# One core, attention then two expert stages: q's tail is loaded a step later and turned into features beside its own attention

## The chip, the cores and the metric

The kernel runs on one core of a Trainium2 chip. The metric is the device time of the whole program in microseconds, the median of three runs. The core has a matrix engine (PE; PEld is its weight load), a vector engine (DVE), an activation engine (ACT), GpSimd (POOL) and a queue engine (SP) that here only issues transfers.

## What is computed

Attention with random features on 2 batches, 8 heads, 576 positions and 64 dimensions (128 features), then a gated layer, then four experts. The attention part, which is the one touched, is:

```python
def phi(x):                       # x is q or k, scaled by D**-0.25
    proj = np.einsum('bhsd,md->bhsm', x, omega)
    h = proj - np.sum(x * x, axis=-1, keepdims=True) / 2.0
    h = h - np.max(h, axis=-1, keepdims=True)
    return np.exp(h) / np.sqrt(m)
kv = np.einsum('bhsm,bhsd->bhmd', k_p, v)
z = np.sum(k_p, axis=2)
num = np.einsum('bhsm,bhmd->bhsd', q_p, kv)
den = np.einsum('bhsm,bhm->bhs', q_p, z)[..., None] + 1e-06
return num / den
# then, on tokens x = attention, heads side by side:
h = (x @ w1) * (x @ w2) @ w3 @ w_out
out = sum over e of p[:, e] * (relu(h @ ew1[e]) @ ew2[e])
```

## The kernel before

Two heads of one batch make a pair; there are eight pairs, numbered 0 to 7, and pairs 0 to 3 are batch 0. Of the 576 positions of a head, 512 are the main part. The 64 that are left, of both batches together, make the tail: 128 rows by 8 heads, one tile for k, one for q, two for v.

The loop from line 514 runs nine steps. In step n the features of pair n are made (`features_k`, `features_q`), pair n-1 is finished (`kv_sums`, `transpose_e`, `attend`, `place`), pair n+1 is transposed (`transpose_kq`) and pair n+2 is loaded. The features of half a pair are one product on PE into a bank `ps_f` (line 279), a maximum on DVE (line 285) and four exponentials on ACT (line 291). Line 316 has the exponentials of pairs 5 to 7, which use `features_halves`. A transposed input goes from the bank `ps_t` to `kT` by DVE or to `qT` by ACT; the features of q (`eq`) are transposed into the one bank `ps_et` and copied to `eT` by ACT.

The tail has its own functions. `tail_k` makes features `ekt` in step 0. `tail_q` (line 489) makes those of q, transposes them and leaves them in `eTt`; it is called in step 1. `attend_tail` (line 458) uses `eTt` after the last pair of each batch, that is in steps 4 and 8. In both raw tiles of the tail, `tail_raw`, the tag is `xs`, which has two buffers and is also the tag of the attention results that `attend` makes.

Beside the attention, under lower priority, each step runs pieces of the table `BESIDE` (line 41): `o` loads one tile of the output weights (`wo`, eight in all, in steps 0 to 2), `f0` to `f7` fold `w3` with `wo` (line 195, from step 2 on; each fold is two transposed halves and twice twelve products), and `w` and `b` are weights and products of the gated layer. Weights lie in memory as 64-bit numbers. `from_f64` loads them into one of three buffers `f64`, and turns them into 32 bits with one ACT instruction (line 93) and two DVE instructions (lines 94 and 95); `split` makes two parts, by ACT (line 80) and by POOL or DVE (line 81).

A scheduler that runs when the program is built sets the order on each engine from the priorities and its own idea of durations. Each engine then runs its list in that order and waits at the head of it.

Of the kernel before, what the change touches and what calls it, by code (L numbers as in the profile page):

```python
# [8 lines left out]
F32 = mybir.dt.float32  # L9
# [36 lines left out]
def attention_moe_kernel(ctx: ExitStack, tc: tile.TileContext, q, k, v, omega, mw1, mw2, mw3, mwo, probs, ew1, ew2, out):  # L46
    nc = tc.nc
    B, H, S, D = q.shape
# [3 lines left out]
    NE, _, EFF = ew1.shape  # L52
    P = 128
    NPAIR = H // 2
    R = 4
# [19 lines left out]
    def bank(tag):  # L75
        return ps_p.tile([P, 512], F32, tag=tag, name="ps_" + tag, bufs=BANKS[tag])
# [31 lines left out]
    def transpose(out, in_, rows=slice(0, P)):  # L108
        return nc.tensor.transpose(out, in_, ident[rows, rows])
# [27 lines left out]
    def load_w12(g):  # L137

        for w, src in enumerate((mw1, mw2)):
            src = src[:, g * P:(g + 1) * P].rearrange("(k p) c -> p k c", p=P)  # L140
            t = load_w64(w1_p, src, "w12", nc.gpsimd)
            w12[w, g] = t.rearrange("p a (k c) -> p a k c", k=KD)

    def load_wo():
        f = len(wo)
        wo.append(load_w64(w1_p, mwo[f * P:(f + 1) * P].unsqueeze(1), "wo", nc.gpsimd))
# [38 lines left out]
    def fold(m):  # L185

        po = bank("po")
        n = 0
        for hf in range(KF // 4):
            u = m * (KF // 4) + hf  # L190
            while len(w3T) < min(u + 2, KF * (KF // 4)):
                fold_transposed(len(w3T))
            for g in range(4):
                for a, c in PASSES:
                    nc.tensor.matmul(  # L195
                        out=po, lhsT=w3T[u][:, a, g * P:(g + 1) * P], rhs=wo[hf * 4 + g][:, c],
                        start=(n == 0), stop=(n == 3 * KF - 1),
                    )
                    n += 1
        t = w3_p.tile([P, 2, 512], F32R, tag="w3o", name="w3o", bufs=KF)  # L200
        split(t[:, HI], t[:, LO], po)
        w3o.append(t)
# [51 lines left out]
    with ExitStack() as actx:  # L254
        at = actx.enter_context(tc.tile_pool(name="at", bufs=2))
# [3 lines left out]
        def transposed(r, name, tag="t"):  # L259

            ps = bank(tag)
            for g in range(4):
                transpose(ps[:, g * P:(g + 1) * P], r[:, 2 * g:2 * g + 2].rearrange("p r d -> p (r d)"))
            t = at.tile([P, 512], F32, tag=name, name=name)
            if name == "kT":
                nc.vector.tensor_scalar(out=t, in0=ps, scalar1=SCALE, scalar2=None, op0=ALU.mult)
            else:
                nc.scalar.activation(out=t, in_=ps, func=ACTF.Copy, scale=SCALE)
            return t
# [3 lines left out]
        def features(t, half, e, tag="f", wide=False):  # L273


            ps = bank(tag)
            for g in range(2):
                c = (half * 2 + g) * P
                nc.tensor.matmul(
                    out=ps[:, g * 256:(g + 1) * 256], lhsT=t[:, c:c + P], rhs=om.rearrange("p j m -> p (j m)"),  # L280
                    start=True, stop=True,
                )
            pv = ps.rearrange("p (g m) -> p g m", m=M)
            mx = at.tile([P, 4], F32, tag="mx", name="mx", bufs=4)
            top = nc.vector.tensor_reduce(out=mx, in_=pv, op=ALU.max, axis=AX.X, negate=True)
            if wide:
                nc.vector.tensor_tensor(out=e, in0=pv, in1=mx.unsqueeze(2).to_broadcast([P, 4, M]), op=ALU.add)
                last = nc.scalar.activation(out=e, in_=e, func=ACTF.Exp)
            else:
                for g in range(4):  # L290
                    last = nc.scalar.activation(out=e[:, g], in_=pv[:, g], func=ACTF.Exp, bias=mx[:, g:g + 1])
            ended.append(last.ins)
            return top.ins, last.ins
# [26 lines left out]
        def load_tail(r, src, b, eng=nc.sync):  # L320
            eng.dma_start(out=r, in_=src[b, :, MAIN:, :].rearrange("h s d -> s h d"))
# [12 lines left out]
        rows_of = [slice(b * TAIL, (b + 1) * TAIL) for b in range(B)]  # L334
# [123 lines left out]
        def attend_tail(b, ps_of):  # L458

            rows = rows_of[b]  # L460
            xs = at.tile([P, H, D], F32, tag="xs", name="xs")
            for f in range(2):
                ps = bank(("x", "kv")[f])
                for g in range(4):
                    h = f * 4 + g
                    nc.tensor.matmul(
                        out=ps[:, g * D1:(g + 1) * D1], lhsT=eTt[:, h], rhs=ps_of[h // 2].kva[:, h % 2],
                        start=True, stop=True,
                    )
                normalised(xs[:, f * 4:(f + 1) * 4], ps, slice(0, P), 4)  # L470
            ps = bank("et")
            s = TAIL_COLS
            for i in range(NPAIR):
                transpose(ps[:, i * P:(i + 1) * P], xs[:, 2 * i:2 * i + 2].rearrange("p j d -> p (j d)"))
            for i in range(NPAIR):
                x, c = xt[b][i], i * P + b * TAIL
                split(x[:, HI, s], x[:, LO, s], ps[:, c:c + TAIL])
# [3 lines left out]
        def pair(n):  # L481
            return pairs[n] if 0 <= n < len(pairs) else None

        def tail_k():
            t = transposed(tail_raw[0], "kT")
            for half in range(2):
                features(t, half, ekt[:, half * 4:half * 4 + 4])

        def tail_q():
            t = transposed(tail_raw[1], "qT")  # L490
            for half in range(2):
                e = at.tile([P, R, M], F32, tag="eq", name="eq", bufs=3)
                features(t, half, e)
                ps = bank("et")
                for g in range(4):
                    transpose(ps[:, g * P:(g + 1) * P], e[:, g])
                nc.scalar.activation(
                    out=eTt[:, half * 4:half * 4 + 4], in_=ps.rearrange("p (g t) -> p g t", g=4), func=ACTF.Copy,
                )

        pairs[0].load_kq(nc.scalar)
        with tc.issue_after(om_first):
            pairs[0].transpose_kq()
        tail_raw = [at.tile([P, 2 * R, D], F32, tag="xs", name="tail") for _ in range(2)]
        for b in range(B):
            load_tail(tail_raw[0][rows_of[b]], k, b)
        pairs[0].load_v()
# [6 lines left out]
        for n in range(len(pairs) + 1):  # L514
            u, u1, nx, nx2 = pair(n), pair(n - 1), pair(n + 1), pair(n + 2)
            with tc.high_priority(offset=-100 if n < 6 else 400):
                if u:
                    u.place_v()
                if n == 0:
                    for b in range(B):  # L520
                        load_tail(tail_raw[1][rows_of[b]], q, b)
                if nx2:
                    nx2.load_kq()
                    nx2.load_v()
                    loaded = nx2.loaded
                if u1:
                    u1.kv_sums()
                if u:
                    u.features_k()
                if u1:  # L530
                    u1.transpose_e(0)
                    u1.transpose_e(1)
                if u:
                    u.features_q()
                if n == 0:
                    tail_k()
                if u1:
                    u1.attend()
                if n == 1:
                    tail_q()  # L540
                if nx:
                    nx.transpose_kq()
                if u1:
                    u1.place()
                    if u1.i == NPAIR - 1:
                        attend_tail(u1.b, pairs[u1.n - u1.i:u1.n + 1])
            with ExitStack() as order:

                for ins in (*u.mark, loaded) if u else ():
                    order.enter_context(tc.issue_after(ins))  # L550
                for s in BESIDE.get(n, "").split():
                    if s[0] == "w":
                        load_w12(int(s[1]))
                    elif s[0] == "o":
                        load_wo()
                    elif s[0] == "f":
                        fold(int(s[1]))
                    else:
                        gated(at, 2, int(s[1]), int(s[2]), ("w", "po") * 2)
# [319 lines left out]
```

## Time and profile before

| what | us |
|---|---|
| median of 3 runs | 675.74 (674.23 to 676.59) |
| profiled execution, own time | 675.28 |
| its span, first to last instruction | 673.5 |
| PE busy in the span | 661.3 (98%) |
| ACT busy | 414.1 (61%) |
| DVE busy | 448.9 (67%) |

The span holds four stages: attention with the weights that are prepared beside it, the folds and the first gated products that join it from 59 us on, the rest of the gated layer, and from about 310 us the experts. A busy share is a mean over stages with different limits. So the rows that count are those of the stage that the change touches, and in it the times at which PE has nothing to do. Busy time of PE is drawn a little long, since the ends of products are modelled; the distance from the start of one row to the start of the next is what tells whether PE ran on.

### The profile page before, as it was taken

Reading aid. Unit: us, or ns where it says so; the run is one execution under the profiler, and the core shown is the slowest. Engines: PE = TensorE matmul, PEld = TensorE weight load, DVE = VectorE, ACT = ScalarE, POOL = GpSimd, SP = SyncE. Lnnn points to the kernel's source line nnn. Section 1 sums busy time; section 2 is a strip of 40 time slices with the busy share of each in tenths; the row PEclk is TensorE's granted clock in tenths of the full one; section 3 lists DMA queues with packets and bytes.
Section 4 is the critical chain, followed back from the end, with each engine's and each line's share of the span. In section 5 each row is a group of like instructions: output and inputs, shape, how many; then the busy total and the mean of one; then the engine's idle time right before and its main releaser. Section 6 shows DMA issues by size and latency. Waiting matters only on the chain.

```text
span 673.5 us, 12392 instructions
## 1 busy us (share of the span) xinstructions
PE 661.3 (98%) x4895; PEld 634.7 (94%) x4895; DVE 448.9 (67%) x754; ACT 414.1 (61%) x895; POOL 123.9 (18%) x145
## 2 busy tenths in 40 slices
PE   8999999999999999999999999999999999999997
PEld 6788888889999999999899999999999998999996
DVE  3867755657462225257968867968689588687795
ACT  5897465574352224237868778768587677687740
POOL 2321000042140000000022141321331312304300
PEclk9999999999999999999999999999999999999999
DMA  9865333156120002002255385592872765737715
GB/s 230 289 204 173 109 111 95 63 176 200 32 64 1 1 1 64 1 1 64 77 143 142 46 145 108 98 154 48 156 142 32 147 120 83 142 75 105 135 44 172
DMA packets 51178, 70.58 MB, mean 105 GB/s; under 512 B 8048, under 2 KB 34160, under 8 KB 51120
## 3 DMA queue, kind: packets, MB, share of 16 engines
q1 hardware_dynamic: 37792, 49.05, 24.3%
q0 software_dynamic: 12640, 20.19, 20.1%
q8 instruction: 38, 0.62, 0.4%
q10 hardware_dynamic: 688, 0.56, 0.2%
q14 instruction: 20, 0.16, 0.1%
HBM read 47.24 MB, written 22.54 MB: 104 GB/s over the span
## 4 chain that ended last, share of the span: by engine, by line
PE 83%; DMA 5%; DVE 4%; issue 3%; ACT 3%; SPq 1%; POOL 0%; DVEq 0%; ACTq 0%; POOLq 0%
PE ps_po L195 6%; PE ps_f L709 6%; PE ps_f L791 5%; PE ps_x L709 3%; PE ps_w L709 3%; PE ps_et L709 3%; PE ps_po L158 3%; PE ps_f L158 3%; PE ps_kv L709 3%; PE ps_po L709 3%; PE ps_kv L791 3%; PE ps_x L791 3%; PE ps_w L158 3%; PE ps_et L791 3%; PE ps_t L709 2%
## 5 line engine op out<-in xcount | busy, mean ns | idle before, releaser
L743 POOL DMA_DIRECT2D out_dram<-o x98 | 81.9, 912 | 355.2 <-DVE o L768 173.0
L81 DVE TENSOR_TENSOR hs<-hd,hs 128x1024 fp32r<-128x1024 f32 x48 | 58.3, 1218 | 1.5 <-ACT hs L80 1.5
L80 ACT ACTIVATE hs<-hd 128x1024 fp32r<-128x1024 f32 x48 | 50.6, 1056 | 5.7 <-DVE hd L605 4.6
L195 PE MATMUL ps_po<-wo,w3T 128*128 128x512 f32 x192 | 48.3, 400 | 0.0
L709 PE MATMUL ps_f<-x,w1e 128*128 128x288 f32 x288 | 46.2, 294 | 0.0
L693 ACT ACTIVATE hd<-hd 128x288 f32<-128x288 f32 x96 | 40.7, 438 | 9.0 <-DVE hd L691 8.5
L605 DVE TENSOR_TENSOR hd<-hd 128x512 f32<-128x512 f32 x64 | 43.9, 686 | 0.8
L605 DVE TENSOR_TENSOR raw<-raw 128x512 f32<-128x512 f32 x64 | 43.9, 686 | 0.5
L791 PE MATMUL ps_f<-w2e,hs 128*128 128x256 f32 x288 | 43.2, 282 | 0.0
L81 DVE TENSOR_TENSOR w2e<-raw,w2e 128x1024 fp32r<-128x1024 f32 x32 | 38.8, 1218 | 5.4 <-ACT w2e L80 5.3
L195 PEld LDWEIGHTS ps_po<-wo,w3T 128*128 128x128 f32 x192 | 34.8, 188 | 7.0
L709 PEld LDWEIGHTS ps_f<-x,w1e 128*128 128x128 f32 x288 | 40.9, 188 | 0.1
L791 PEld LDWEIGHTS ps_f<-w2e,hs 128*128 128x128 f32 x288 | 38.5, 191 | 0.1
L80 ACT ACTIVATE w2e<-raw 128x1024 fp32r<-128x1024 f32 x32 | 33.1, 1054 | 6.3 <-DVE raw L605 3.2
L81 POOL TENSOR_TENSOR w<-w12f,w 128x512 fp32r<-128x512 f32 x16 | 23.5, 1478 | 68.0 <-ACT w L80 68.0
L81 DVE TENSOR_TENSOR w1e<-raw,w1e 128x1024 fp32r<-128x1024 f32 x24 | 29.3, 1219 | 5.8 <-ACT w1e L80 5.7
L158 PE MATMUL ps_po<-xt,w 128*128 128x288 f32 x144 | 32.5, 296 | 0.4 <-DVE w3o L81 0.4
L158 PE MATMUL ps_w<-xt,w 128*128 128x288 f32 x144 | 32.8, 297 | 0.0
L80 ACT ACTIVATE hid<-a 128x288 fp32r<-128x288 f32 x32 | 12.8, 439 | 28.8 <-DVE a L169 28.8
L80 ACT ACTIVATE w1e<-raw 128x1024 fp32r<-128x1024 f32 x24 | 25.4, 1058 | 6.2 <-issue 2.6
L94 DVE TENSOR_SCALAR f64e<-f 128x512 uint32<-128x512 uint32 x40 | 20.6, 520 | 8.4 <-DMA f<-in_moe_w_dram 5.5
L158 PE MATMUL ps_x<-xt,w 128*128 128x288 f32 x96 | 25.8, 297 | 0.0
(272 smaller groups left out, 1769.2 us busy)
## 6 DMA issues: line engine op xcount, KB each, us to landing
f<-in_moe_w_dram SPq DMA_DIRECT2D x32, 512.0 KB, 3.8
raw<-in_moe_w_dram SPq DMA_DIRECT2D x32, 512.0 KB, 5.2
out_dram<-o POOLq DMA_DIRECT2D x56, 256.0 KB, 5.3
out_dram<-o POOLq DMA_DIRECT2D x42, 128.0 KB, 4.8
f<-in_moe_w_out_dram SPq DMA_DIRECT2D x8, 512.0 KB, 6.2
kr<-in_k_dram SPq DMA_DIRECT2D x8, 256.0 KB, 5.3
vr<-in_v_dram SPq DMA_DIRECT2D x8, 256.0 KB, 4.9
o<-out_dram SPq DMA_DIRECT2D x8, 256.0 KB, 3.8
```

The lines of the kernel that those rows point to most:

```text
L80: nc.scalar.activation(out=hi, in_=src, func=ACTF.Copy)
L81: (eng or nc.vector).tensor_tensor(out=lo, in0=src, in1=hi.bitcast(F32), op=ALU.subtract)
L94: nc.vector.tensor_scalar(out=e, in0=low, scalar1=29, scalar2=None, op0=ALU.logical_shift_right)
L158: nc.tensor.matmul(out=bs[c][:, :HS], lhsT=w12[w, g][:, x, kk], rhs=xt[b][kk][:, y, c * HS:(c + 1) * HS], start=(kk == 0 and n == 0), stop ...
L195: nc.tensor.matmul(out=po, lhsT=w3T[u][:, a, g * P:(g + 1) * P], rhs=wo[hf * 4 + g][:, c], start=(n == 0), stop=(n == 3 * KF - 1),)
L605: nc.vector.tensor_tensor(out=o, in0=x, in1=y, op=op)
L693: nc.scalar.activation(out=h, in_=src, func=ACTF.Relu)
L709: nc.tensor.matmul(out=ps, lhsT=w1t[a][:, x, kk, g * P:(g + 1) * P], rhs=x2[b, kk][:, y, s], start=(k in "125" and kk == 0 and n == 0), st ...
L743: dma = nc.gpsimd.dma_start(out=out[toks, d], in_=src[rows], **({} if fresh else dict(accum_op=ALU.add))).ins
L791: nc.tensor.matmul(out=ps, lhsT=t[a][:, x, g, j * P:(j + 1) * P], rhs=w2t[b][:, y, g], start=(k in "15" and g == 0 and n == 0), stop=(k in ...
```

## The change

The raw tile of q's tail gets a tag of its own, `tailq`, with one buffer. Its two loads move from step 0 to step 1, behind the loads of pair 3. `tail_q` moves from step 1 to step 4 (`n == NPAIR`), ahead of `attend` of pair 3 and of the first `attend_tail`. No instruction is added or taken away; the scheduler makes a new order from it.

```diff
-        tail_raw = [at.tile([P, 2 * R, D], F32, tag="xs", name="tail") for _ in range(2)]
+        tail_raw = [at.tile([P, 2 * R, D], F32, tag=tag, name="tail", bufs=n) for tag, n in (("xs", 2), ("tailq", 1))]
...
-                if n == 0:
-                    for b in range(B):
-                        load_tail(tail_raw[1][rows_of[b]], q, b)
                 if nx2:
                     nx2.load_kq()
                     nx2.load_v()
                     loaded = nx2.loaded
+                if n == 1:
+                    for b in range(B):
+                        load_tail(tail_raw[1][rows_of[b]], q, b)
...
                 if n == 0:
                     tail_k()
+                if n == NPAIR:
+                    tail_q()
                 if u1:
                     u1.attend()
-                if n == 1:
-                    tail_q()
```

The order on ACT from the split of pair 0's result (`xt_75`) on; `wof` and `wo` are weights, `ek` and `eq` exponentials. Before:

```order
L80 ACTIVATE xt_75<-ps_x 128x512
L291 ACTIVATE eq<-ps_f,mx 128x128 x4
L93 ACTIVATE wof<-f_430 128x512
L93 ACTIVATE wof<-f_440 128x512
L291 ACTIVATE eq<-ps_f,mx 128x128 x4
L80 ACTIVATE wo<-wof 128x512
L268 ACTIVATE qT<-ps_t 128x512
L80 ACTIVATE wo<-wof 128x512
L497 ACTIVATE eTt<-ps_et 128x512
L291 ACTIVATE eq<-ps_f,mx 128x128 x4
L291 ACTIVATE ek<-ps_f,mx 128x128 x4
```

The same place of the change:

```order
L80 ACTIVATE xt_75<-ps_x 128x512
L291 ACTIVATE eq<-ps_f,mx 128x128 x4
L93 ACTIVATE wof<-f_391 128x512
L93 ACTIVATE wof<-f_401 128x512
L438 ACTIVATE eT<-ps_et 128x512
L291 ACTIVATE ek<-ps_f,mx 128x128 x4
L80 ACTIVATE wo<-wof 128x512 x2
L438 ACTIVATE eT<-ps_et 128x512
L291 ACTIVATE ek<-ps_f,mx 128x128 x4
L291 ACTIVATE eq<-ps_f,mx 128x128 x4
L268 ACTIVATE qT<-ps_t 128x512
```

The tail's two sets of exponentials and its `eTt` copies are gone from here, and pair 1's transposed features (`eT`) and pair 2's exponentials come in their place.

The order on PE from the first transposition of `w3` (`w3f`) to the first fold (L195). Before:

```order
L109 MATMUL ps_w<-ident,w3f 128x128 x4
L109 MATMUL ps_t<-ident,kr 128x128 x4
L279 MATMUL ps_f<-om,kT 128x256 x2
L109 MATMUL ps_x<-ident,xs 128x128 x4
L429 MATMUL ps_kv<-va_116,ek 128x65 x4
L429 MATMUL ps_kv<-vt_119,ekt 128x65
L429 MATMUL ps_kv<-va_116,ek 128x65 x4
L429 MATMUL ps_kv<-vt_119,ekt 128x65
L109 MATMUL ps_et<-ident,eq 128x128 x3
L109 MATMUL ps_w<-ident,w3f 128x128 x4
L195 MATMUL ps_po<-wo,w3T 128x512 x12
```

Of the change:

```order
L109 MATMUL ps_w<-ident,w3f 128x128 x4
L109 MATMUL ps_t<-ident,kr 128x128 x4
L279 MATMUL ps_f<-om,kT 128x256 x2
L109 MATMUL ps_et<-ident,eq 128x128 x4
L279 MATMUL ps_f<-om,qT 128x256 x2
L445 MATMUL ps_x<-kva,eT 128x65 x4
L109 MATMUL ps_t<-ident,qr 128x128 x4
L445 MATMUL ps_kv<-kva,eT 128x65 x4
L109 MATMUL ps_w<-ident,w3f 128x128 x4
L195 MATMUL ps_po<-wo,w3T 128x512 x12
L279 MATMUL ps_f<-om,qT 128x256 x4
```

Pair 3's attention (L445) now stands ahead of the first fold, where it stood behind it; the tail's features follow behind the first fold.

The order on DVE and SP where the experts' probabilities (`pr`, `prs`) are handled. SP before, from `f_840` on, then SP of the change, from `f_770` on, then DVE of the change:

```order
L87 DMA f_840<-in_moe_w_dram 128x1024
L391 DMA vr<-in_v_dram 128x2x256
L87 DMA f_867<-in_moe_w_dram 128x1024
L580 DMA pr<-in_moe_domain_probs_dram 128x4 x4
L580 DMA pr<-in_moe_domain_probs_dram 64x4 x2
L580 DMA pr<-in_moe_domain_probs_dram 128x4 x4
```

```order
L87 DMA f_770<-in_moe_w_dram 128x1024
L391 DMA vr<-in_v_dram 128x2x256
L580 DMA pr<-in_moe_domain_probs_dram 128x4
L87 DMA f_801<-in_moe_w_dram 128x1024
L580 DMA pr<-in_moe_domain_probs_dram 128x4 x3
L380 DMA qr<-in_q_dram 128x2x256
L580 DMA pr<-in_moe_domain_probs_dram 64x4 x2
L580 DMA pr<-in_moe_domain_probs_dram 128x4 x2
L87 DMA f_828<-in_moe_w_dram 128x1024
L580 DMA pr<-in_moe_domain_probs_dram 128x4 x2
```

```order
L581 TENSOR_REDUCE prs<-pr 128x9
L582 TENSOR_SCALAR prs<-prs 128x9
L583 RECIPROCAL prs<-prs 128x9
L584 TENSOR_TENSOR pr<-pr,prs 128x36
L81 TENSOR_TENSOR xt_78<-ps_x,xt_78 128x512
L81 TENSOR_TENSOR w3T<-ps_w,w3T 128x512
L95 SCALAR_TENSOR_TENSOR w3f<-w3f,f64e 128x512
L94 TENSOR_SCALAR f64e<-f_828 128x512
L266 TENSOR_SCALAR kT<-ps_t 128x512
L81 TENSOR_TENSOR w3o<-ps_po,w3o 128x512
```

The last two probability loads stand behind a weight load that they stood ahead of, and the four `pr` instructions of DVE stand ahead of the third `w3T` split and the first `w3o` split of the folds.

## Rows read from the trace of the kernel before

**Rows 1.** Part 1 of the page: busy us, share, instructions.

```profile
PE 661.3 (98%) x4895; PEld 634.7 (94%) x4895; DVE 448.9 (67%) x754; ACT 414.1 (61%) x895; POOL 123.9 (18%) x145
```

**Rows 2.** Windows by stage: busy us of each engine (x instructions), clock, DMA share, GB/s.

```profile
20.63:27.73 7.10, 6.35 (x49) 5.86 (x48) 6.53 (x13) 5.52 (x18) 3.63 (x3) 1.00 1.01 339
27.73:35.10 7.37, 6.17 (x32) 4.38 (x32) 5.50 (x9) 7.37 (x23) 3.43 (x4) 1.00 0.69 201
59.04:145.38 86.34, 86.34 (x589) 75.24 (x588) 53.29 (x117) 48.84 (x123) 5.13 (x6) 1.00 0.34 102
```

**Rows 3.** Chain of waits, 20 to 60 us: start us, us, what.

```profile
28.82 1.03 ACT eq L291 x4
29.85 1.11 ACT wof L93 x2
30.96 1.03 ACT eq L291 x4
...
44.88 5.91 DMA f<-in_moe_w_dram
...
53.13 0.92 PE ps_f L279 x4
```

**Rows 4.** Timeline of PE: start us, us, line, out<-in, xcount, [idle <-releaser].

```profile
26.38 0.60 PE L109 MATMUL ps_x<-ident,xs 128*128 128x128 f32 x4
27.73 1.13 PE L279 MATMUL ps_f<-om,qT 128*128 128x256 f32 x4 [0.75 <-ACT eq L291]
28.70 0.60 PE L109 MATMUL ps_t<-ident,kr 128*128 128x128 f32 x4
29.91 1.13 PE L279 MATMUL ps_f<-om,qT 128*128 128x256 f32 x4 [0.61 <-ACT eq L291]
...
43.50 1.00 PE L445 MATMUL ps_po<-kva,eT 128*128 128x65 f32 x8
44.34 0.61 PE L109 MATMUL ps_et<-ident,eq 128*128 128x128 f32 x4
44.78 1.03 PE L279 MATMUL ps_f<-om,kT 128*128 128x256 f32 x4
45.65 1.03 PE L279 MATMUL ps_f<-om,qT 128*128 128x256 f32 x4
...
50.38 0.84 PE L109 MATMUL ps_et<-ident,eq 128*128 128x128 f32 x3 [0.22 <-ACT eq L291]
52.05 1.08 PE L445 MATMUL ps_x<-kva,eT 128*128 128x65 f32 x8 [0.83 <-DVE xt L81]
...
59.04 3.00 PE L195 MATMUL ps_po<-wo,w3T 128*128 128x512 f32 x12
```

**Rows 5.** Timeline of ACT where the tail of q is worked.

```profile
33.33 0.68 ACT L497 ACTIVATE eTt<-ps_et 128x512 f32<-128x512 f32 x1
33.82 1.22 ACT L291 ACTIVATE eq<-ps_f,mx 128x128 f32<-128x128 f32 x4
34.82 1.25 ACT L291 ACTIVATE ek<-ps_f,mx 128x128 f32<-128x128 f32 x4
```

**Rows 6.** Timeline of POOL and DVE: two instructions together, then the second kind alone.

```profile
20.95 1.27 POOL L81 TENSOR_TENSOR wo<-wof,wo 128x512 fp32r<-128x512 f32 x1 [2.12 <-ACT wo L80]
21.02 1.75 DVE L95 SCALAR_TENSOR_TENSOR wof<-wof,f64e 128x512 uint32<-128x512 uint32 x1
...
60.63 0.68 DVE L95 SCALAR_TENSOR_TENSOR w3f<-w3f,f64e 128x512 uint32<-128x512 uint32 x1
```

**Rows 7.** Timeline of SP and DVE: a `w3` load's issue, its first use.

```profile
43.67 0.34 SPq L87 DMA_DIRECT2D f<-in_moe_w_dram  x1
...
48.05 0.57 DVE L94 TENSOR_SCALAR f64e<-f 128x512 uint32<-128x512 uint32 x1 [0.67 <-DMA f<-in_moe_w_dram]
```

**Rows 8.** Timeline of SP and DVE: the probability loads, their first use.

```profile
60.88 5.38 SPq L580 DMA_DIRECT2D pr<-in_moe_domain_probs_dram  x10
...
67.69 0.18 DVE L581 TENSOR_REDUCE prs<-pr 128x9 f32<-128x36 f32 x1
```

## The prediction

> **What bounds the kernel now.** I read part 1 of the page first: PE is busy for 98% of the span [rows 1], so a change that takes no work from PE can only win where PE stands still, and can win no more than that. The second view is the windows by stage. From 59.04 us, where the first fold starts, to 145.38 us PE is busy for 86.34 of 86.34 us [rows 2]: folds fill every hole there. Ahead of it PE stands still, and ACT does not: from 27.73 to 35.10 us ACT is busy for 7.37 of 7.37 us [rows 2]. The third view, the chain of waits, says the same in order of time. Around 30 us it runs through ACT, one set of exponentials behind the other; one later piece is a weight load of 5.91 us; from 53 us on it stays on PE [rows 3].
>
> The fourth view, PE's timeline, gives the size of the holes. Where nothing is waited for, four transpositions move PE on by 0.44 us (44.34 to 44.78), half a set of features by 0.87 us (44.78 to 45.65), four of the small attention products by 0.84 us (43.50 to 44.34) [rows 4]. Against these, the start at 27.73 is 0.91 us late (26.38 + 0.44 = 26.82), the one at 29.91 is 0.77 us late. There are seven such holes between 26.38 and 52.05: 0.91, 0.77, 0.41, 0.75, 0.34, 0.45 and, the last one, 1.34 us (50.38 and three transpositions of 0.11 each, to 52.05) [rows 4]. Their sum is 4.97 us. That is what can be had here; earlier holes lie ahead of the place where the two orders part.
>
> **The change, part by part.** *What leaves.* On ACT the tail of q is one copy to `qT`, two copies to `eTt` and two sets of exponentials. A set moves ACT on by 1.00 us (33.82 to 34.82) and a copy by 0.49 us (33.33 to 33.82) [rows 5]; together 2 x 1.00 + 3 x 0.49 = 3.5 us, most of it between 30.77 and 37 us. On PE it is 12 transpositions and 4 feature products: 12 x 0.11 + 2 x 0.87 = 3.1 us [rows 4]. This work is not gone; it goes behind the first fold.
>
> The trace has 1.22 us for such a set but 1.00 us to the next start, so four exponentials overlap in part [rows 5]. The Trainium skill, "ScalarE: Activation LUTs", section "What ACT_TABLE_LOAD costs", has the price of one ACTIVATE and an overlap of about 93 ns between neighbours; for 128 elements with a bias per row an estimate from that page is 0.39 - 0.09 = 0.29 us, 1.18 us a set and 3.9 us for the whole. By that page the relief would be 0.4 us larger, and the time below up to 0.4 us lower; the row is 0.25 us apiece, and I go by the row.
>
> *What that gives.* ACT is where PE's feature work waits, and the tail asks more ACT for its PE time (3.5 to 3.1) than the folds do, beside which it now lies. In the fold stage ACT is busy for 48.84 of 86.34 us [rows 2], so there it is covered; without that cover it would cost its 3.5 us. On PE it costs nothing either way, since each product runs once. What counts is thus the holes that are left ahead of the first fold.
>
> I laid the changed rows of ACT, DVE and PE end to end from 20 us on, with the spacings above, 0.55 us for a weight conversion on ACT (29.85 to 30.96 for two, [rows 3]), and each row behind what it reads. The order on PE ahead of the first fold has nearly the same work as before: 11 transpositions and one feature product fewer (11 x 0.11 + 0.43), 8 attention products more (8 x 0.21), 0.1 us in all by these spacings, 0.3 us by finer ones. Four holes above 0.1 us are left. First, pair 2's second half of k features waits for pair 1's second exponentials: PE is ready at 29.55, ACT at 30.1, hole 0.55. Second, the transposition behind it needs the bank `ps_et`, which the copy `eT` empties at 31.65, behind two weight conversions on ACT; PE is ready at 31.0, hole 0.65. Third, pair 3's first q features wait at 41.8 for exponentials that end at 42.85, hole 1.1. Fourth, 0.25 us in small pieces around 45 to 47 us. The sum is 2.55 us against 4.97: **-2.4 us**.
>
> *What this leaves out.* A start behind a wait costs PE some more: the feature row at 27.73, which waited, took 0.97 us to the next start instead of 0.87 [rows 4]. For four such starts that is +0.4 us. And the weights have to be there. A conversion frees the buffer that a later load waits for. In the new order the first `w3` load waits for the sixth `wo` conversion, which stands behind pair 2's exponentials, and so leaves at about 40.3 us. The load issued at 43.67 was used at 48.05, 4.4 us later, after DVE had waited 0.67 us for it [rows 7]; another took 5.91 us [rows 3]. So it lands at 44.7 to 46.2 us, and in the new order its conversion stands on DVE ahead of the maximum of pair 3's q features, which is ready at about 44.0. Behind that maximum are the exponentials, the transposition and PE. ACT has other work until 45.85 us, which covers 1.2 us of the delay: 0 to +1.0 us, and I take +0.5.
>
> *The loads of the tail* (256 KB) go behind two of pair 2's on SP and stay ahead of the weight loads, so no weight moves for them. The tile of its own frees a buffer of `xs`; nobody waits for `xs` in the holes above, so nothing is counted for it. `tail_q` late asks for buffers of `eq`, of which there are three: its second half waits for pair 4's features to be transposed. Folds stand around it on PE, and its result is wanted by gated products only at about 145 us; cost nothing.
>
> The sum: -2.4 + 0.4 + 0.5 = **-1.5 us**. From the profiled execution's 675.28 us that is 673.8 us; the median of the runs is 0.46 us above that execution, so 675.74 - 1.5 = **674.2 us**. A measurement of this kernel can tell about 0.3%, 2.0 us, from no change; the forecast lies inside it, near the edge.
>
> **The rivals.** *Fuller gain.* If ACT's list runs as closely as the spacings say, the load lands early and the two small additions are nil, it is -2.4 us. If also the 1.1 us hole closes, because ACT reaches pair 3's exponentials sooner, it is -3.4 us: 672.3 to 673.7 us. For it: ACT is full exactly where the tail stood [rows 2]. Against: 2.55 us of holes that do not depend on the tail are left.
>
> *No gain.* The weights' path stays the limit. The two-input conversion on DVE took 1.75 us beside a split on POOL that began 0.07 us earlier [rows 6], and 0.68 us alone [rows 6], so such a meeting costs about 1.0 us. If the late `w3` load meets the splits of `wo` that POOL makes at about 43 to 46 us, and once more at an earlier pair of conversions, 2 x 1.0 us comes back to -1.5: 674.8 to 676.7 us. The Trainium skill, "SBUF — State Buffer", section "SBUF: two separate sides", has VectorE and GpSimd share a port pair that one of them holds for a whole instruction while the other blocks; by that rule each meeting could cost the whole 1.27 us of the split instead of 1.0, and the time would be up to 0.5 us higher still. The row agrees: 1.20 us of the split were left, and 1.20 + 0.68 is 1.88 against 1.75.
>
> *Slower.* The four `pr` instructions of DVE now stand ahead of the third `w3T` split and the first `w3o` split, and their last two loads stand on SP behind a weight load. In the kernel before the ten loads took SP 5.38 us and DVE used them 1.4 us after the last issue, at 67.69 [rows 8], with no split held up. In the new order I find the last loads issued at about 59 us, in use at 61 to 62 us, and the third fold half needs its split at about 67 us, so the block is covered with more than a microsecond to spare. It decides from the point where `f_828`, ahead of the last two, waits for its buffer some 5 us longer than that. Then SP, DVE and the folds stand, and PE loses 2 to 4 us more than the gain: -1.5 + 4 = +2.5, 678.2 us. For it: SP waits on many of these buffers. Against: the conversion that frees this one needs only the second transposition of `w3`, ahead of the first fold.
>
> **How the numbers follow.** Forecast, -0.9 to -2.0 us: 0.42. Fuller gain: 0.31. No gain, -0.7 to +1.0 us: 0.15. Slower: 0.12. The forecast's far end touches the edge of 0.3%, so 0.04 of it goes to faster: faster 0.35, same 0.53, slower 0.12. The range for 8 in 10 goes from the end of the fuller gain, 675.74 - 3.4 = 672.3, over no gain to the beginning of the slower case, 676.9 us; outside stay most of the slower case and a small part on the low side.
>
> **What would show it.** In the profile of the changed kernel the first L195 row should start at 57 to 58 us instead of 59.04, the holes of PE from 26 to 52 us should sum to about 3.0 to 3.5 us instead of 4.97, with the longest in front of pair 3's q features, and PE should have no hole from there to 145 us. ACT should show no `eTt` copy until after the first fold. The last `prs` instruction should end before 64 us without a wait behind it. The forecast is wrong if the first L195 starts no earlier than 58.7 us, or if holes turn up among the folds between 60 and 145 us; and if the first L195 starts 1.5 us earlier and the end does not, the later stages have taken it back, which no row here suggests.

## The result, and the profile of the changed kernel

The change makes the kernel **slower**: 679.84 us (median of six runs, 679.21 to 682.05) against 675.91 us for the kernel before in the same series (674.23 to 677.03), a ratio of 1.0071 with a 95% interval of 1.0057 to 1.0084. The forecast was 674.2 us and the range ended at 676.9. The profiled execution took 680.21 us, its span is 678.4 us, 4.9 us more than that of before.

PE's line in part 1 of the page hardly differs from [rows 1]; it says that the work is the same, not where time went:

```profile
PE 662.1 (98%) x4895; PEld 634.6 (94%) x4895; DVE 447.5 (66%) x754; ACT 412.9 (61%) x895; POOL 122.9 (18%) x145
```

To place the 4.9 us I cut both spans at the same rows of PE: pair 0's first attention product (L445 into `ps_w`), the first fold (L195), the first gated product (L158), the last row. The first of them, in the timeline of PE of before and then of the change:

```profile
20.63 1.00 PE L445 MATMUL ps_w<-kva,eT 128*128 128x65 f32 x8
```

```profile
22.38 1.00 PE L445 MATMUL ps_w<-kva,eT 128*128 128x65 f32 x8
```

The windows between first fold, first gated product and last row, of the change (columns as in [rows 2], whose last row is the first window of before):

```profile
57.87:148.55 90.68, 88.00 (x575) 74.41 (x574) 51.75 (x114) 50.97 (x130) 4.70 (x5) 1.00 0.34 103
148.55:672.42 523.87, 520.99 (x3975) 514.51 (x3974) 356.53 (x560) 318.78 (x642) 100.59 (x112) 1.00 0.43 90
```

and the last of these windows of before:

```profile
145.38:668.98 523.60, 519.91 (x3963) 513.26 (x3962) 355.25 (x557) 318.73 (x642) 101.82 (x112) 1.00 0.43 90
```

| stretch | before | after | difference |
|---|---|---|---|
| start to the L445 row | 20.63 | 22.38 | +1.75 |
| to the first fold | 38.41 | 35.49 | -2.92 |
| folds, to the first gated product | 86.34 | 90.68 | +4.34 |
| to the last row of PE | 523.60 | 523.87 | +0.27 |
| last row of PE to the end of the span | 4.52 | 5.98 | +1.46 |

So the stretch that the change was about gained what the prediction reckoned with and more. Three others lost: the start, the folds and the very end.

The holes ahead of the first fold are those of [rows 4] no longer; in PE's timeline of the change these are left:

```profile
31.39 1.13 PE L279 MATMUL ps_f<-om,kT 128*128 128x256 f32 x4
32.98 0.66 PE L109 MATMUL ps_et<-ident,eq 128*128 128x128 f32 x4 [0.46 <-ACT eT L438]
...
41.74 1.03 PE L279 MATMUL ps_f<-om,kT 128*128 128x256 f32 x4
42.97 0.66 PE L109 MATMUL ps_et<-ident,eq 128*128 128x128 f32 x4 [0.20 <-ACT eT L438]
44.49 1.13 PE L279 MATMUL ps_f<-om,qT 128*128 128x256 f32 x4 [0.86 <-ACT ek L291]
```

With the prediction's spacings they are 0.72, 0.36 and 1.08 us (31.39 + 0.87 to 32.98, and so on); with one of 0.30 ahead of 31.39 the sum is 2.46 us, against 4.97.

Among the folds, where before had no hole above 0.25 us, PE now stands four times for 0.4 us or more. The first place, in the timelines of SP, DVE and PE of the change:

```profile
61.59 0.36 SPq L87 DMA_DIRECT2D f<-in_moe_w_dram  x1
62.00 0.90 SPq L580 DMA_DIRECT2D pr<-in_moe_domain_probs_dram  x2
```

```profile
65.83 0.19 DVE L581 TENSOR_REDUCE prs<-pr 128x9 f32<-128x36 f32 x1 [2.42 <-DMA pr<-in_moe_domain_probs_dram]
...
67.23 0.68 DVE L81 TENSOR_TENSOR w3T<-ps_w,w3T 128x512 fp32r<-128x512 f32 x1
...
68.89 0.68 DVE L266 TENSOR_SCALAR kT<-ps_t 128x512 f32<-128x512 f32 x1
```

```profile
67.39 0.38 PE L109 MATMUL ps_et<-ident,eq 128*128 128x128 f32 x2
67.97 0.66 PE L109 MATMUL ps_w<-ident,w3f 128*128 128x128 f32 x4 [0.20 <-DVE w3T L81]
68.46 0.38 PE L109 MATMUL ps_et<-ident,eq 128*128 128x128 f32 x2
69.63 0.66 PE L109 MATMUL ps_t<-ident,qr 128*128 128x128 f32 x4 [0.78 <-DVE kT L266]
70.23 0.50 PE L195 MATMUL ps_po<-wo,w3T 128*128 128x512 f32 x1
```

DVE stands 2.42 us at the head of its list for the last probability load, which SP had issued by 62.90 and DVE could use 2.9 us later; the bank copies behind it (`w3T`, `kT`) come late, and PE stands 0.36 + 0.95 + 0.16 us (0.22, 0.22 and 0.44 us are two, two and four transpositions).

The second place has no wait in it. Ten microseconds on, PE's timeline reads:

```profile
78.53 0.49 PE L303 MATMUL ps_f<-omh,kT 64*128 64x128 f32 x4
78.95 0.43 PE L466 MATMUL ps_x<-kva,eTt 128*128 128x65 f32 x2
79.32 0.49 PE L303 MATMUL ps_f<-omh,kT 64*128 64x128 f32 x2
79.73 0.44 PE L466 MATMUL ps_x<-kva,eTt 128*128 128x65 f32 x2
80.10 0.49 PE L303 MATMUL ps_f<-omh,kT 64*128 64x128 f32 x2
...
81.57 0.39 PE L466 MATMUL ps_kv<-kva,eTt 128*128 128x65 f32 x2
```

Products of `attend_tail` (L466, on all 128 rows) alternate with pair 5's features (L303, on 64 rows). A pair of each kind takes 0.78 us (79.32 to 80.10); where they stand apart (below) two L303 take 0.14 and two L466 0.21 us. The cost is not that of any two kinds in turn: at 34.31 to 36.74 us of the same trace L429, L279 and L109, all with 128 rows, take turns and lose at most 0.05 us a change.

Two more holes follow where before had none: two sets of transpositions into the one bank `ps_et` back to back (0.90 us), and a product behind a transposition that waits for DVE's `xs` (0.75 us); one more, of 0.54 us, waits for `w3o` at 89 us:

```profile
106.45 0.60 PE L109 MATMUL ps_et<-ident,eq 128*128 128x128 f32 x4
107.79 0.66 PE L109 MATMUL ps_et<-ident,eq 128*128 128x128 f32 x4 [0.74 <-ACT eT L438]
...
114.87 0.61 PE L109 MATMUL ps_et<-ident,eq 128*128 128x128 f32 x4
116.06 1.08 PE L429 MATMUL ps_kv<-va,ek 128*128 128x65 f32 x8 [0.58 <-DVE xs L364]
```

From row to row PE loses 6.4 us against undisturbed spacings in this stage, 1.1 us in the kernel before.

### The profile page after: what moved, and what is told of

Read it like the earlier page. It is cut to its first block, busy times and chain, and to the rows that moved or that the text cites. A ratio compares the mean times of both kernels' runs of the same rounds, so it can differ in the third digit from the quotient of the medians.

```text
span 678.4 us, 12388 instructions
## 1 busy us (share of the span) xinstructions
PE 662.1 (98%) x4895; PEld 634.6 (94%) x4895; DVE 447.5 (66%) x754; ACT 412.9 (61%) x895; POOL 122.9 (18%) x145
## 3 DMA queue, kind: packets, MB, share of 16 engines
q1 hardware_dynamic: 37792, 49.05, 23.9%
HBM read 47.24 MB, written 22.54 MB: 103 GB/s over the span
## 4 chain that ended last, share of the span: by engine, by line
PE 83%; DMA 4%; DVE 4%; ACT 4%; issue 3%; SPq 0%; POOL 0%; DVEq 0%; POOLq 0%; ACTq 0%
PE ps_po L195 6%; PE ps_f L709 6%; PE ps_f L791 5%; PE ps_x L709 3%; PE ps_w L709 3%; PE ps_et L709 3%; PE ps_w L158 3%; PE ps_f L158 3%; PE ps_po L158 3%; PE ps_kv L709 3%; PE ps_po L709 3%; PE ps_kv L791 3%; PE ps_x L791 3%; PE ps_et L791 3%; PE ps_t L709 2%
## 5 line engine op out<-in xcount | busy, mean ns | idle before, releaser
L195 PE MATMUL ps_po<-wo,w3T 128*128 128x512 f32 x192 | 48.8, 401 | 0.4 <-DVE w3o L81 0.4
L709 PE MATMUL ps_f<-x,w1e 128*128 128x288 f32 x288 | 46.2, 294 | 0.0
L195 PEld LDWEIGHTS ps_po<-wo,w3T 128*128 128x128 f32 x192 | 34.6, 188 | 7.6 <-DVE w3o L81 0.8
L158 PE MATMUL ps_w<-xt,w 128*128 128x288 f32 x144 | 34.9, 297 | 0.0
L158 PE MATMUL ps_po<-xt,w 128*128 128x288 f32 x144 | 34.6, 296 | 0.0
L158 PE MATMUL ps_x<-xt,w 128*128 128x288 f32 x96 | 25.5, 297 | 0.0
```

The costliest lines, as they stand in the source:

```text
L158: nc.tensor.matmul(out=bs[c][:, :HS], lhsT=w12[w, g][:, x, kk], rhs=xt[b][kk][:, y, c * HS:(c + 1) * HS], start=(kk == 0 and n == 0), stop ...
L195: nc.tensor.matmul(out=po, lhsT=w3T[u][:, a, g * P:(g + 1) * P], rhs=wo[hf * 4 + g][:, c], start=(n == 0), stop=(n == 3 * KF - 1),)
L709: nc.tensor.matmul(out=ps, lhsT=w1t[a][:, x, kk, g * P:(g + 1) * P], rhs=x2[b, kk][:, y, s], start=(k in "125" and kk == 0 and n == 0), st ...
```

## The experiments

All ratios are against runs of the kernel before on the same chip, in the same series. "End" is the time from the last row of PE to the end of the profiled span.

| run | what it is | ratio (95%) | end |
|---|---|---|---|
| `after_again` | the change | 1.0065 (1.0043 to 1.0087) | 5.9 |
| `before_again` | the kernel before | 1.0006 (0.9985 to 1.0027) | 4.5 |
| `load_late` | later loads alone | 1.0003 (0.9984 to 1.0022) | 4.5 |
| `work_late` | later work alone | 1.0052 (1.0035 to 1.0069) | 6.0 |
| `prs5` | change, `prs` out of the way | 1.0025 (1.0011 to 1.0039) | 4.5 |
| `low` | change, `attend_tail` at low priority | 0.9995 (0.9978 to 1.0013) | 4.5 |
| `alt` | change, no alternation | 1.0016 (0.9999 to 1.0032) | 4.5 |
| `low_prs5` | change, `low` and `prs5` | 0.9979 (0.9965 to 0.9993) | 4.5 |
| `wl_low_prs5` | `work_late`, `low` and `prs5` | 0.9966 (0.9948 to 0.9984) | 4.5 |
| `before_low` | before, `low` | 1.0011 (0.9995 to 1.0026) | 4.5 |
| `before_low_prs5` | before, `low` and `prs5` | 1.0014 (0.9999 to 1.0029) | 5.9 |
| `work_3` | change, `tail_q` in step 3 | 0.9979 (0.9961 to 0.9996) | 4.5 |
| `pad_dve` | change, 16 more DVE instructions | 1.0039 (1.0017 to 1.0060) | 4.5 |
| `pad_dve4` | change, 4 more | 1.0030 (1.0009 to 1.0051) | 4.5 |

The difference of two of these ratios carries both intervals, about 0.25% or 1.8 us; where less is at stake, the traces decide.

**The two parts of the change, apart.** Four kernels: both parts, none, the loads alone, the work alone.

> The changed kernel once more. In its first profiled execution the rows were 2.0 us late by 20 us already (the granted clock was 0.69 in 10:12 and 0.50 in 12:14), ahead of the place where the orders of PE part, and then another 3 us were lost among the folds. Theory A (the folds): the 3 us of the folds belong to the order and come again, the slip at the start was chance: span about 676.5 us, first L195 at 56 us, first L158 at 146.5. Theory B (the start too): by another order of loads the clock falls again in 10:14 and all rows from 20 us on stand 2 us late as in the first execution: span 678.4, first L195 at 57.9, first L158 at 148.5.

> The kernel before once more, for what differs from one execution to the next without any change. If the start slips by chance, some executions of this kernel should show it too, and its rows should then stand up to 2 us apart from those of the first trace; if it doesn't, the granted clock is 1.00 in 10:14 and the first L195 starts at 59.0 us within 0.2 us, span 673.5.

`load_late` is the diff of the change without its last two hunks, `work_late` the diff without its first two (both have the tile of its own).

> The loads alone: the own tile and the later loads of q's tail, with its features and transposes left in step 1. All engines but SP keep the order of the kernel before; on SP the loads of pair 2 stand ahead of those of the tail. Theory A: nothing waits for these loads, 0.0 us within 0.5 (ratio 0.999 to 1.001). Theory B (the order of loads starves PE at the start): the 2 us of the start come here, 677.9 us, ratio 1.003.

> The work alone: the own tile, features and transposes in step 4, but the loads of q's tail in step 0 as before. PE, ACT, DVE and POOL have the order of the changed kernel; SP has the tail's loads ahead of pair 2's. Theory A (the loss is in the folds, by the order on PE, DVE and ACT): the first L195 about 3 us earlier than before (56 us), 6.3 us of holes from there to 148 us instead of 1.7, and the end 1 to 3 us later than before: 677 to 679 us, ratio 1.002 to 1.005. Theory B (the loads make 2 us of it): 2 us less than the changed kernel, ratio 1.004 to 1.005 to the kernel before. If the changed kernel and this one agree within 0.1%, the place of the loads does not matter.

The loads do nothing (1.0003); the work makes the loss (1.0052, which agrees with the 1.0065 of both within the intervals). Its fold window:

```profile
57.66:148.38 90.72, 87.99 (x575) 74.44 (x574) 51.76 (x114) 50.93 (x130) 4.71 (x5) 1.00 0.34 103
```

90.72 us, as in the change (90.68). Theory B of the start fell: in `after_again` the granted clock was 1.00 from 10 to 14 us, and its L445 row stands at 19.64 us, earlier than in the first trace of before. Over all executions profiled that row lies between 19.64 and 21.69 with the order of before and between 19.64 and 22.54 with the later work: the start scatters by 2 us, and the +1.75 of the table is not the change's. The rest holds: from the L445 row to the first fold `after_again` took 35.76 us, `before_again` 38.63.

**The wait for the probabilities.** In `prs5` the four instructions are held behind pair 5's features of q; only DVE's order differs from that of the change.

```diff
+        for ins in pairs[5].mark:
+            order.enter_context(tc.issue_after(ins))
         nc.vector.tensor_reduce(out=prs, in_=pr, op=ALU.add, axis=AX.X)
```

> The changed kernel with one thing moved: the four prs instructions of DVE stand behind the weight conversion f64e<-f_1309, some 30 us later; PE, ACT, POOL and SP keep their order. In the trace of the change DVE stands 2.42 us at the first of them for the last probability load, and behind it PE has holes of 0.36, 0.95 and 0.16 us from 67.4 to 70.2 us. Theory A (this wait is a cause): these 1.5 us close, 1.0 to 1.5 us less than the changed kernel, ratio to the kernel before 1.004 to 1.005. Theory B (DVE has enough slack there and PE waits for ACT anyway): no change within 0.5 us, ratio 1.006 to 1.007.

0.40% less than the change, 2.7 us give or take 1.8, more than either theory. PE's timeline at the place shows what theory A said: the hole at `qr` is 0.15 us instead of 0.95, that at `w3f` is gone.

```profile
66.24 0.60 PE L109 MATMUL ps_w<-ident,w3f 128*128 128x128 f32 x4
66.67 0.38 PE L109 MATMUL ps_et<-ident,eq 128*128 128x128 f32 x2
67.04 0.66 PE L109 MATMUL ps_t<-ident,qr 128*128 128x128 f32 x4
```

The holes there sum to 0.30 us instead of 1.47, which is 1.2 us. The end is 1.4 us shorter as well; it is taken up last. Together they make 2.6 of the 2.7. The whole fold window of this profile is no shorter (91.10 us): in this execution PE's granted clock fell during one fold, which took 4.43 us instead of 2.84 (last section). Without those 1.6 us it is 1.2 us shorter than the change's 90.68, which is what the holes give.

**The alternation.** `low` moves `attend_tail` out of its step's high priority, `alt` only holds pair 5's products behind the first tail product.

```diff
-                    if u1.i == NPAIR - 1:
-                        attend_tail(u1.b, pairs[u1.n - u1.i:u1.n + 1])
+            if u1 and u1.i == NPAIR - 1:
+                attend_tail(u1.b, pairs[u1.n - u1.i:u1.n + 1])
```

> The changed kernel with attend_tail called at the end of its step under the low priority, so that its products (L466) no longer alternate with the 64-row products of pair 5's features (L303). In the trace of the change each of seven alternations between 74 and 82 us costs PE 0.15 to 0.27 us, 1.4 us in all, and two sets of four transpositions into the one bank ps_et stand back to back at 106 us, 0.90 us. Theory A (the interleaving is a cause): 1.4 to 2.3 us less than the changed kernel, ratio to the kernel before 1.003 to 1.0045. Theory B (only the waits for DVE count): no change, 1.006 to 1.007.

```diff
             with ExitStack() as order:
+                order.enter_context(tc.issue_after(tails[0]))
                 for c in range(R):
```

> The changed kernel with pair 5's 64-row products (L303) held behind the first product of attend_tail, so that the two kinds no longer alternate; up to there all engines keep the order of the changed kernel, behind it the order shifts locally up to the gated products. Theory A (the alternation costs PE its 0.15 to 0.27 us each time): about 1.4 us less than the changed kernel, ratio to the kernel before 1.004 to 1.005, the wait of DVE for the probability loads and its holes still there. Theory C (the gain of the low priority came from the other places that it shifted): no change, 1.006 to 1.007.

> Both edits in the changed kernel. If the two causes are separate and make up the loss among the folds, the gains add: 2.5 to 3.8 us less than the changed kernel, ratio to the kernel before 1.000 to 1.003; with the 3 us gained ahead of the first fold kept, it could come out at 0.999. If something else holds the folds (the preparation of w3 by ACT and DVE), the holes move to other places and the ratio stays above 1.004.

`low` gives 0.70% (4.7 us), `alt` 0.49% (3.3 us). 1.4 us of each is again the end; the rest, 3.3 and 1.9 us, is over the 1.4 to 2.3 that was expected for `low` and near the 1.4 for `alt`. Theory B fell. Theory C would not fall by the ratio alone, since without the end `alt` is 1.9 us off, which is about its uncertainty; the trace decides. There the alternation is gone, the holes behind the probabilities are not (0.57 and 0.95 us), and the fold window is 88.19 us, 2.5 less than the change's; in `low` it is 89.46, of which about 1.4 us is a fall of the clock. Both edits together go **below the kernel before** (0.9979). The groups by line in the window from 70 to 84 us, first of the change, then of `low_prs5`; the columns are busy time and mean ns of one:

```profile
L303 PE MATMUL ps_f<-omh,kT 64*128 64x128 f32 x16 | 2.7, 316 | 0.0
L466 PE MATMUL ps_x<-kva,eTt 128*128 128x65 f32 x8 | 1.7, 300 | 0.0
```

```profile
L303 PE MATMUL ps_f<-omh,kT 64*128 64x128 f32 x16 | 1.2, 285 | 0.0
L466 PE MATMUL ps_x<-kva,eTt 128*128 128x65 f32 x8 | 1.0, 268 | 0.0
```

The same 24 instructions fill 4.4 us of PE when they alternate and 2.2 us when they don't (2.3 in `alt`). No wait is shown, and PE reads as busy. In PE's timeline of `low_prs5` each kind is one row:

```profile
75.04 1.00 PE L466 MATMUL ps_x<-kva,eTt 128*128 128x65 f32 x8
75.88 0.39 PE L109 MATMUL ps_et<-ident,eq 128*128 128x128 f32 x2
...
76.85 1.16 PE L303 MATMUL ps_f<-omh,kT 64*128 64x128 f32 x16
77.95 3.02 PE L195 MATMUL ps_po<-wo,w3T 128*128 128x512 f32 x12
```

The Trainium skill has this rule ("TensorEngine Tiling (Array Packing)", section "Key Properties"): a change of the tiling mode drains TensorE. The trace agrees in so far as each of the seven changes between 64 and 128 rows costs 0.14 to 0.27 us; that it is a drain no view here shows. And the whole fold window of `low_prs5` has one PE instruction more than that of the change and is 5.0 us shorter:

```profile
57.77:143.42 85.65, 85.01 (x576) 73.46 (x574) 51.42 (x114) 51.09 (x131) 5.17 (x5) 1.00 0.37 110
```

**Controls.** Do the two edits gain without the later work, does the place of the loads matter with them, and does another place of the work lose too?

> The kernel before with attend_tail under the low priority: whether that edit gains by itself. There the products L303 and L466 do not alternate, and PE loses 1.1 us in all from 59 to 147 us, so there is little to gain: ratio 0.999 to 1.001. If it is below 0.998, the gain of the edit in the changed kernel says nothing on the change.

> The two edits in the kernel before, as a control. If the 0.9979 of the changed kernel with both edits comes from the tail's later work, the two edits alone give 0.999 to 1.001 here; below 0.998 they gain by themselves and the later work has nothing to do with it.

> The later work with both edits, but the loads of q's tail in step 0, as in the kernel before. The place of the loads made no difference with the kernel before (0.0003), so this should agree with the changed kernel with both edits: ratio 0.997 to 0.999. If it is at 1.000 or above, the load's place matters once the folds no longer hide it.

> The changed kernel with tail_q in step 3 instead of 4. In this order the tail's products and transposes stand ahead of the first fold, attend_tail does not alternate with pair 5's products, and the prs instructions stand behind the third split of w3T, as in the kernel before. Theory A (the loss is in these two places alone): the folds lose about as little as before (1.1 us) and the result lies at 0.998 to 1.001. Theory D (any later place of the work delays the folds): 1.003 or more.

In the kernel before the edits gain nothing (1.0011, 1.0014). The second ratio has the long end in it, 1.4 us; without it, it would be 0.9993, and the intervals around that and around 0.9979 overlap. I therefore compare the profiles without start and end, from the L445 row to the last row of PE: 645.4 to 645.9 us in `low_prs5`, `wl_low_prs5` and `work_3`, 649.3 in `before_low_prs5`, 647.4 to 649.0 in `before`, `before_again` and `load_late`, 650.0 to 650.7 in the change, `work_late` and `pad_dve4`. (Profiles in which the granted clock fell behind that row are left out.) So the 0.9979 comes from the later work. The loads' place does not matter (0.9966, an interval that overlaps). `work_3`, one number changed (`n == 3`), has no alternation and gives 0.9979. DVE still waits 2.30 us for the probabilities there, but behind the third `w3T` split, and PE has one hole after it, 0.52 us, in which it waits for a `w3o`. Theory D fell: a later place as such costs the folds little. `wl_low_prs5` and `work_3` both beat both kernels; their intervals overlap.

**The end.** After the last row only the last stores are left, and they take 1.4 us longer in the change. The transfers in its last 4.9 us, then those in the last 4.5 us of the kernel before (part 3 of the transfer view; the last line's numbers are the size and the time from issue to landing):

```profile
q14 instruction: 1, 0.01, 0.9%
issues: line engine op xcount, KB each, median us to landing
out_dram<-o SPq DMA_DIRECT2D x1, 256.0 KB, 3.5
```

```profile
q1 hardware_dynamic: 349, 0.62, 37.0%
issues: line engine op xcount, KB each, median us to landing
out_dram<-o SPq DMA_DIRECT2D x2, 256.0 KB, 2.1
```

A load of instructions (queue q14) lies among the packets of the last store, which takes 3.5 us to land instead of 2.1. It does so in the four profiles with an end of 5.9 to 6.0 us and in none of the other ten. If q14 carries DVE's instructions, more of them ahead should move that load:

```diff
+    with tc.issue_after(pairs[-1].mark[0]):
+        [nc.vector.memset(zeros[:, 2 * i:2 * i + 2], 0.0) for i in range(16)]
```

> The changed kernel with 16 more DVE instructions (zeros written into a tile that nobody reads any more), in the gated stage, where DVE has time; the order of all else is that of the changed kernel. In the three profiles of that order the last instruction load of queue q14 falls among the packets of the last store, and from the last PE row to the end of the span it takes 5.9 to 6.0 us; in ten profiles of other orders that load came earlier or not at all and it was 4.5 to 4.6 us. Theory E (q14 loads DVE's instructions and that load holds up a packet of the store): the load moves ahead of the store, the end takes 4.5 to 4.6 us, the median falls by 1.4 us to a ratio of 1.004 to 1.005. Theory F (the end is long for another reason of this order): 5.9 us and 1.006 to 1.007.

> The same with 4 instructions instead of 16. In the last microseconds DVE starts a row every 0.7 to 0.8 us, so by theory E the load moves 1 to 3 us earlier, to 671.5 to 674.5 us: at the front of the last store or just ahead of it, so that the end takes anything from 4.5 to 6.0 us. By theory F it is 5.9 us.

Both give an end of 4.5 us and 1.0039 and 1.0030: theory E. The load begins at 668.8 us in `pad_dve`, 9.3 us ahead of the end of its span, at 668.9 in `pad_dve4`, 5.5 us ahead, and at 675.6 in the change, 2.8 us ahead. The intervals touch that of the change (1.0043 to 1.0087), so the end of the span is the clearer sign; by the medians 4 to 16 instructions that do nothing take 1.8 to 2.4 us off.

## Why the prediction was wrong

**What bounds the kernel: right.** PE's holes ahead of the first fold are ACT's, and the tail's work on ACT makes them. From the same row to the first fold the change takes 35.49 us against 38.41. In seven more profiles of this order it took 35.5 to 35.8 us (36.78 in `work_late`), with the order of before 38.63 in `before_again` and 37.15 in `load_late`; so 2.7 us is a fair size, though `load_late` against most of the others gives 1.4, and against `work_late` 0.4.

That is the rival of the fuller gain; the forecast's -1.5 was too small by most of the +0.4 for starts behind a wait (0.1 us at the start at 44.49, the same at 48.64) and by the +0.5 for weights that come late. The load did come late: DVE waited 1.00 us for it and used it at 45.73, within the 44.7 to 46.2 forecast, but ACT's other work covered it, and PE's next hole is of 0.2 us.

The list laid end to end was good to a tenth in its largest entry: 1.1 us ahead of pair 3's q features (1.08), 0.65 us at `ps_et` (0.72), 0.55 at pair 2's k features (0.30), 0.25 in pieces (0.36, in one piece). The first L195 stands at 57.87, within the 57 to 58 forecast, but only because the start was late by chance; in `after_again` it is 55.40. The meeting of DVE and POOL, the mechanism of "no gain", did not happen: each two-input conversion from 20 us to the first fold took at most 0.7 us. The sum of 4.97 us is a little low: with three transpositions in the row at 34.32, as the trace has it, and 0.84 us for the eight attention instructions at 49.05, those two holes are 0.45 and 0.49 us and the seven make 5.1.

**"On PE it costs nothing either way, since each product runs once": the step that failed.** It counts products and not their neighbours. `tail_q` late pushes `attend_tail` beside pair 5's features, the first ones made with 64 rows, and two kinds that stood apart now change places seven times: 1.4 us from row to row (0.14 + 3 x 0.27 + 3 x 0.16), 2.2 us of busy time by the groups, 1.9 us in `alt` by the ratios. The busy share that the prediction read, 86.34 of 86.34 us, could not show such a loss: in the change PE reads as busy for 88.00 us of this stage with 14 instructions fewer. The order on PE around it was there to be read before the run; the trace of before even had the price, since its 64-row products there are split by four transpositions, and the six ahead of them take 0.64 us to the next row where six undisturbed ones take 0.41:

```profile
68.89 0.71 PE L303 MATMUL ps_f<-omh,kT 64*128 64x128 f32 x6
69.53 0.66 PE L109 MATMUL ps_w<-ident,w3f 128*128 128x128 f32 x4
70.12 0.93 PE L303 MATMUL ps_f<-omh,kT 64*128 64x128 f32 x10
```

"Folds stand around it; cost nothing" fell for the same reason: where transpositions into the one bank `ps_et` meet, folds did not stand between (0.90 us behind the row at 106.45).

**Slower: the right place, the wrong trigger.** The four `prs` instructions at the head of DVE's list do stop it, and the holes behind them are those named (`w3T`, `kT`). The rival made it depend on a buffer: SP waiting some 5 us at `f_828`. SP did not wait there; it issued the last loads by 60.26 us in `after_again` (forecast: about 59). The 2.9 us until they landed, and the start of the folds 2 us earlier than reckoned, used up the margin of "more than a microsecond": in use at 63.16, forecast 61 to 62. The step was read as covered with a landing time that no row of the group showed, since before used the loads [rows 8] without a wait. Its price, 2 to 4 us, was too high for itself (1.2 us in `prs5`); that it is about right for the folds as a whole (+4.3) is luck, since the alternation and the other holes make up the rest.

**What was not in the sum.** The end, +1.4 us, from where an instruction load falls. Part of the whole loss (3.9 us by the medians of the first series, 4.8 by its ratio, 4.4 by that of `after_again`) stays unexplained: -2.9, +4.3, +0.3 and +1.4 make +3.1 us. The scatter between executions is of the size of the rest; no run settles it.

**The signs to watch.** "No PE hole from there to 145 us" and "the last `prs` before 64 us without a wait" were the two that named the loss, and both turned out wrong. No `eTt` copy before the first fold: right. Holes of 3.0 to 3.5 us ahead of it, the longest at pair 3's q features: right in the place, 2.46 in the sum.

With the two places mended the change gives the number that the forecast said: 0.9979 is -1.4 us, with an interval of -2.4 to -0.5 (forecast: -1.5). That the two agree so well is partly luck. Ahead of the first fold it gains 2.7 us and not 1.5, and some of the -1.4 is that none of its 12 executions had a fall of the clock (last section), against 10 of 35 of the kernel before; by the medians of the executions without one, 673.50 and 674.29 us, it is -0.8.

## What to carry to other kernels

When a scheduler re-sorts a full engine, look in the new order for neighbours, not only for waits: alternating 64-row and 128-row products cost PE twice their time and read as busy. An instruction that needs a small, late transfer is a plug at the head of its engine's list; give it a place well behind its data. A gain of 0.4% in one stretch is only worth something if the stretch that takes over the work is read row by row too.

## What was not expected of the hardware

An instruction load can hold up a store: 1.4 us at the end of the kernel, when one transfer of queue q14 (20 of them, 0.16 MB in all, so 8 KB each) fell among the last store's packets, and nothing in the twelve profiles where it fell elsewhere. The Trainium skill ("Runtime: NRT & Kernel Launch", section "Instruction fetch mechanics") has each engine's sequencer fetch its instructions through a DMA queue of its own, in blocks of 16 KiB, at a cost that is mostly hidden. The queue of its own agrees with `pad_dve`; the blocks of q14 are of 8 KB here (those of q8, the other instruction queue, are of 16: 38 in 0.62 MB), and at the last store the cost is not hidden.

The granted clock of PE falls once in some executions, of the kernel before too, to 0.50, which is the lower of its two levels (1.2 GHz), for 3 to 7 us, and PE loses 1.4 to 3 us. It was at 10 to 14 us in the first trace of the change, behind waits of 0.74 to 1.25 us. In `after_again`, `prs5` and `pad_dve`, three of the five other profiles with the alternation, it came right behind it, in the products of the next fold. The windows of `after_again` (columns as in [rows 2], the clock third from the end):

```profile
77.00:79.00 2.00, 2.00 (x13) 1.60 (x12) 1.85 (x4) 0.45 (x3) 0.00 (x0) 1.00 0.37 78
79.00:81.00 2.00, 2.00 (x8) 1.62 (x7) 1.89 (x6) 0.78 (x4) 0.00 (x0) 0.60 0.49 184
81.00:83.00 2.00, 2.00 (x6) 1.57 (x5) 0.00 (x0) 0.00 (x0) 0.00 (x0) 0.55 0.00 0
```

PE is shown as busy throughout; the twelve products of that fold took 4.42 us (4.43 in the two others) instead of 2.84:

```profile
79.05 4.58 PE L195 MATMUL ps_po<-wo,w3T 128*128 128x512 f32 x12
83.47 0.33 PE L466 MATMUL ps_kv<-kva,eTt 128*128 128x65 f32 x2
```

In `low` it came at 69.2 to 72.6 us, behind holes of 1.06 and 0.95 us. The changed order does not bring these falls more often. Every profiled execution with a fall has a mean granted clock of 0.997 or less, and none without one has; by that mark 14 of 54 executions of the six kernels that alternate had a fall and 34 of 116 of the kernel before. In `low_prs5`, `wl_low_prs5` and `work_3` it is 2 of 36. Why those have fewer is open.
